# Load order, scratch of the cross products, and the last output rows of a gated long-convolution and MLP kernel

## The chip, the cores and the metric

The kernel runs on one core of one Trainium2 chip. The metric is device time in microseconds (us): the median of four runs, 191.75 us, with single runs from 191.6 to 191.89. Lower is better.

The core has a matrix engine (TensorE, PE in the profile; its weight loads are listed as PEld), VectorE (DVE), ScalarE (ACT), GpSimd (POOL), a queue engine that issues most transfers (SyncE, SP) and 16 DMA engines. Matrix products land in PSUM and are read from there by ScalarE or VectorE; everything else lies in SBUF.

## The reference

There are 2048 positions with 640 channels each. The output mixes two branches with a gate per position: `g * a + (1 - g) * b`.

```
g = sigmoid(sum(q * gate_w, channels))

# branch a: short filter, product, long convolution, product
k_shift = 4-tap causal filter of k over positions, own taps per channel
kv      = k_shift * v
y       = causal convolution of kv with ssm_k (2048 taps per channel) + kv * ssm_D
a       = q * y

# branch b: a two-layer MLP over the positions, per channel
h = layernorm(q over channels)
u = gelu(h^T @ w1 + b1)          # 2048 positions -> 1536
b = (u @ w2 + b2)^T              # 1536 -> 2048 positions
```

All inputs and the output are bf16. The reference does the long convolution by a Fourier transform of twice the length.

## The kernel before, in words

**Branch a.** The positions are split by residue: position 4r + p belongs to residue p, and the 2048 positions to four blocks `hk` of 512, two per half h. The long convolution is done in a transformed domain. TensorE multiplies the filter and the product kv by tables of sines and cosines (`FTB`, filled by ScalarE from integer angles that VectorE prepares in `pint`); ScalarE copies each result out of PSUM into a spectrum tile `C[0]` to `C[3]`, with `SS` as a further half tile. VectorE combines the residues (`mixing`), multiplies spectra, combines again (`invmix`), and TensorE multiplies by the transposed tables `GTB` (`inverse`). ScalarE scales the result by the gate into one of three `cgb` buffers; VectorE multiplies by q and adds the MLP branch, which is already in `O1`; a transfer stores the rows.

**The filter's way in.** `ssm_load(hk)` loads one 640 KB block of the filter, `x_load(hk)` one 640 KB block of q. `transp(h, p, kt)` transposes the filter on TensorE in 16 groups of five 128x128 products, and ScalarE evicts each to `wT`. The very first group also folds in the row `ssm_D`. `fwd` then makes the spectra from `wT`. The 4-tap filter's taps are transposed in a group named `cst`, evicted by ScalarE into `cw` in four pieces, and GpSimd makes `KF` from `cw`.

**Branch b.** Layer normalisation statistics and scaling of q are VectorE work (GpSimd supplies the reciprocal root). The first layer is 12 output tiles of 64 products (`m1`), each followed by a gelu on ScalarE; the second is 16 tiles of 24 products (`m2`), in the block order 2, 3, 0, 1. Each `m2` tile is evicted by ScalarE with scale `omg` (that is 1 - g) and bias `c2` (that is (1 - g) * b2) into `O1`. The very last tile (block 1, residue 3) goes through its first 320 channels before its last 320, so that the two halves can leave PSUM one after the other.

**The spectral products.** The product of half 1's output needs two terms: the cross product of half 1's data with half 0's filter and the other way round. `cross(g)` makes, for each of two spectra, a product into the scratch `T1` (the tile `tm[1]`), a temporary in `tm[0]`, two results in place, and a transfer on GpSimd's queue that adds the temporary into the first result while it moves. `y1(g)` calls `product`, which uses all of `tm[0]` (as `T0`) and `tm[1]` (as `T1`), and sends two more adding transfers. Half 0's two products follow with the same scratch. Before these, `mixing(C[3], C[2], 0)` works in place on `C[3]` and leaves the data in slots 2 and 3; slots 0 and 1 are later the scratch of half 1's `invmix` (`C3a`).

**What sets the order.** The program adds every operation to a planner (`_Sched`) in program order. The planner finds dependencies from the memory regions read and written. `run` then simulates the engines with fixed costs: an engine that is free takes the ready operation with the lowest `prio`, which is the operation's index unless one is given (0 means at once; `m1` and `m2` chunks of 8 products have very high numbers and fill gaps). Loads on one queue share one rate of 320 GB/s and are due 2 us after they have moved; the adding transfers on GpSimd's queue get 1.2 us to issue and 5 us after they have moved. Each PSUM tile is a `_VT`, which takes one of four PSUM slots from its first product to its last eviction; the convolution class may hold three, the MLP class two. An eviction that depends on something outside its tile hands that dependency to the tile's first product. The planned order is then written out, engine by engine, and a tracker adds the semaphore waits; on the chip the order of each engine is fixed, but the times are not the planner's. Loads marked `chain=True` keep program order.

Lines in the profile are mostly those of helpers: L293 is every matrix product, L666 every ScalarE operation, L622 every two-operand VectorE or GpSimd operation, L636 and L637 operations with a scalar, L870 and L872 the statistics, L267 plain transfers, L262 adding transfers, L260 transposing transfers. Tile names tell them apart (`pp` is PSUM).

Of the kernel before, what the change touches and what calls it, by code (L numbers as in the profile page):

```python
# [12 lines left out]
ACT = mybir.ActivationFunctionType  # L13
ALU = mybir.AluOpType
# [308 lines left out]
class _Sched:  # L323
# [171 lines left out]
    def emit(self):  # L495
        for op in self.order:
            op.emit(None if op.vt is None else self.slots[op.vt.slot])
# [12 lines left out]
def _build(nc, A_q, A_k, A_v, A_shift_k, A_ssm_k, A_ssm_D, B_x, B_w1, B_b1, B_w2, B_b2, gate_w, out):  # L510
# [10 lines left out]
    with ExitStack() as es:  # L521
# [8 lines left out]
        SC = _Sched(T, pp)  # L530
# [21 lines left out]
        def V(h, off, dims, p0=0, pn=128):  # L552
            row = T.mem[h.name][2]
            return bass.AP(tensor=h, offset=p0 * row + off, ap=[[row, pn]] + [list(d) for d in dims])
# [74 lines left out]
        def ts(eng, o, a, s1, s2, op0, op1=None, mode=1, prio=None, extra=0.0):  # L629
            n = n_of(o)  # L630
            d = dve_dur(n, mode) + extra if eng == "DVE" else n / 900.0 + 0.2
            rr = [a] + [x for x in (s1, s2) if isinstance(x, bass.AP)]

            def f(e):
                if s2 is None:
                    return e.tensor_scalar(o, a, s1, None, op0=op0)  # L636
                return e.tensor_scalar(o, a, s1, s2, op0=op0, op1=op1)  # L637
            o_ = SC.add(eng, d, lambda s: T.op(eng, f, rr, [o]), rr, [o], prio=prio, name="ts")
            o_.lock = eng == "POOL" or mode > 1
            return o_  # L640
# [8 lines left out]
        def act(o, i, func, bias=None, scale=None, acc=None, vt=None, prio=None, name="act"):  # L649
            kw = {}  # L650
            rr = []
            nap = 0
            for k_, v_ in (("bias", bias), ("scale", scale)):
                if v_ is not None:
                    kw[k_] = v_
                    if isinstance(v_, bass.AP):
                        rr.append(v_)
                        nap += 1
            ww = [o]
            if acc is not None:  # L660
                kw["accum_out"] = acc
                ww.append(acc)

            def emit(s):
                src = i(s) if vt is not None else i
                return T.op("ACT", lambda e: e.activation(o, src, func, **kw), rr + [src], ww)  # L666
            return SC.add("ACT", act_dur(n_of(o), nap), emit, rr if vt is not None else rr + [i], ww, prio=prio, vt=vt, name=name)

        def evac_dve(o, i, vt, prio=None):
# [2 lines left out]
                return T.op("DVE", lambda e: e.tensor_copy(o, src), [src], [o])  # L672
            return SC.add("DVE", dve_dur(n_of(o), 1), emit, [], [o], prio=prio, vt=vt, name="evd")

        def memset(eng, ap, val, prio=None):
            return SC.add(eng, 0.2, lambda s: T.op(eng, lambda e: e.memset(ap, val), [], [ap]), [], [ap], prio=prio)

# [29 lines left out]
        def dr(t, off, ap):  # L707
            return bass.AP(tensor=t.tensor, offset=t.offset + off, ap=ap)
# [7 lines left out]
        def chk(ci):  # L716
            return lambda s: s[:, ci * 512:ci * 512 + 320]

        def ssm_load(hk):
            dma(ssm[:, :, 512 * hk:512 * hk + 512], dr(A_ssm_k, 512 * hk, [[S, 128], [128 * S, ND], [1, 512]]), 128 * ND * 1024, chain=True)  # L720

        def x_load(hk):
            dma(X[:, hk, :, :], dr(A_q, 512 * hk * D, [[4 * D, 128], [1, 4 * D]]), 128 * 5120, chain=True)
# [23 lines left out]
        def small(o, i, nbytes, stream, **kw):  # L747
            dma(o, i, nbytes, stream=stream, **kw)
# [2 lines left out]
        small(rows[0:4, 1, :], dr(B_b2, 0, [[512, 4], [1, 512]]), 4096, "QA")  # L751
        small(rows[0:12, 2, 0:128], dr(B_b1, 0, [[128, 12], [1, 128]]), 3072, "QA")
        small(Drow[:, :], dr(A_ssm_D, 0, [[0, 1], [1, D]]), 1280, "QA")
        x_load(0)
        for hk in range(2):
            ssm_load(hk)
        for hk in range(1, 4):
            x_load(hk)
        ssm_load(2)
# [242 lines left out]
                        act(gb[:, b, :], gb[:, b, :], ACT.Copy, acc=gacc[:, t:t + 1], name="gsum")  # L1002

        tt("DVE", gth[:, :], sd[:, :], gacc[:, :], ALU.mult, mode=1, prio=0)
        ts("DVE", gpre[:, :], mv[:, :, 0], gws[:, 0:1], None, ALU.mult, mode=1, prio=0)
        tt("DVE", gpre[:, :], gpre[:, :], gth[:, :], ALU.add, mode=1, prio=0)
        act(gth[:, :], gpre[:, :], ACT.Tanh, scale=0.5, prio=0)
        ts("DVE", gg[:, :], gth[:, :], 0.5, 0.5, ALU.mult, ALU.add, mode=1, prio=0)
# [4 lines left out]
            dma(GTB[:, p, :, :, :, :].rearrange("q a b c d -> q (a b c) d"), FTB[:, p, :, :, :, :].rearrange("q a b c d -> q (a b c) d"), 128 * 2048, rate=200.0, transpose=True, prio=10 ** 5)  # L1013

        HORD = (2, 3, 0, 1)
        for kt in range(2):
            dma(q_hi[:, kt, :, :], dr(A_q, (1024 + 512 * kt) * D, [[4 * D, 128], [1, 4 * D]]), 128 * 5120)
        for n_, hk in enumerate(HORD):
            W2h = W2[n_ % 2]
            for a in range(2):  # L1020
                w2last = dma(W2h[:, 6 * a:6 * a + 6, :], dr(B_w2, a * 6 * 128 * S + 512 * hk, [[S, 128], [128 * S, 6], [1, 512]]), 128 * 6144)
            for p in range(4):
                vt = _VT("mlp")
                t = 4 * hk + p
                last_ = n_ == 3 and p == 3
                order = [(ft, ci) for ci in range(2) for ft in range(FT)] if last_ else [(ft, ci) for ft in range(FT) for ci in range(2)]
                na = 2 if last_ else 3
                for a in range(na):
                    items = []
                    for ft, ci in order[a * (24 // na):(a + 1) * (24 // na)]:  # L1030
                        items.append((chk(ci), V(W2h, ft * 512 + p, [[4, 128]]), GT[:, ft, 320 * ci:320 * ci + 320], ft == 0, ft == FT - 1))
                    mms(vt, items, prio=2 * 10 ** 6 + 4 * (4 * n_ + p) + a, name="m2")
                    if last_:
                        act(O1[:, hk, p, 320 * a:320 * a + 320], chk(a), ACT.Identity, bias=c2[:, t:t + 1], scale=omg[:, t:t + 1], vt=vt, name="o1")
                if not last_:
                    act(O1[:, hk, p, :].rearrange("p (a b) -> p a b", a=2), two, ACT.Identity, bias=c2[:, t:t + 1], scale=omg[:, t:t + 1], vt=vt, name="o1")

# [44 lines left out]
        def cross(g):  # L1082
            for i in range(2):
                n_ = ncr[0]
                ncr[0] += 1
                tmp = V(tm[0], 1280 * (n_ % 4), [[1, 1280]])
                tt("DVE", half(T1, n_ % 2), half(A0[g], i), half(V1[g], i, True), ALU.mult)
                tt("DVE", tmp, comp(A0[g], i, 1), comp(V1[g], i, 1), ALU.mult)
                tt("DVE", comp(V1[g], i, 0), comp(A0[g], i, 0), comp(V1[g], i, 0), ALU.mult)
                tt("DVE", comp(V1[g], i, 1), comp(T1, n_ % 2, 1), comp(T1, n_ % 2, 0), ALU.subtract)  # L1090
                dma(comp(V1[g], i, 0), tmp, 128 * 5120, stream="POOL", prio=0, accum=True)
# [24 lines left out]
        def inverse(h, Z):  # L1116
            for p in (0, 2, 1, 3):
                hz, sz = Z[p]
                cg = cgb[ncg[0] % len(cgb)]
                ncg[0] += 1  # L1120
                for kt in range(2):
                    t = 8 * h + 4 * kt + p
                    vt = _VT("cv")
                    items = []
                    for k2 in range(2):
                        for c in range(2):
                            for ci in range(2):
                                items.append((chk(ci), GTB[:, p, kt, c, k2, :], V(hz, sz * SL + (2 * c + k2) * D + 320 * ci, [[1, 320]]),
                                              k2 == 0 and c == 0, k2 == 1 and c == 1))
                    mms(vt, items, name="inv")  # L1130
                    act(cg[:, kt, :].rearrange("p (a b) -> p a b", a=2), two, ACT.Copy, scale=gg[:, t:t + 1], vt=vt, name="cg")
                ov = O1[:, 2 * h:2 * h + 2, p, :]
                tt("DVE", cg[:, :, :], cg[:, :, :], (q_lo if h == 0 else q_hi)[:, :, p, :], ALU.mult)
                if h == 0 and p == 3:
                    tt("DVE", O1[:, 0, p, :], cg[:, 0, :], O1[:, 0, p, :], ALU.add)
                    dma(dr(out, p * D, [[4 * D, 128], [1, D]]), O1[:, 0, p, :], 128 * 1280, sem="out")
                    for ci in range(2):
                        ov = O1[:, 1, p, 320 * ci:320 * ci + 320]
                        tt("DVE", ov, cg[:, 1, 320 * ci:320 * ci + 320], ov, ALU.add)
                    ov = O1[:, 1, p, :]  # L1140
                    dma(dr(out, (512 + p) * D, [[4 * D, 128], [1, D]]), ov, 128 * 1280, sem="out")
                else:
                    tt("DVE", ov, cg[:, :, :], ov, ALU.add)
                    dma(dr(out, (1024 * h + p) * D, [[4 * D, 128], [512 * D, 2], [1, D]]), ov, 256 * 1280, sem="out")
# [54 lines left out]
```

## Time and profile before

| | us |
|---|---|
| median of four runs | 191.75 |
| the profiled execution | 191.78 |
| its span, first to last instruction | 190.0 |
| TensorE busy | 176.2 |
| VectorE busy | 170.3 |
| ScalarE busy | 116.8 |
| GpSimd busy | 33.5 |

The profile shows one execution, so sums over it are made against 191.78 and 190.0. The granted TensorE clock was full throughout. "Busy" is an average over stages with different limits: an engine at 90% can still be off the path that sets the end, and what a change is worth has to be read from the stage in which it lies. An idle time in front of an instruction is put down to the semaphore that came last.

### The profile page before, as it was taken

The numbers are of one execution on the slowest core, as the hardware profiler recorded it, in microseconds if no ns is written. First come the engines' busy times: TensorE is split into PE (matmuls) and PEld (weight loads), VectorE is DVE, ScalarE is ACT, GpSimd is POOL, SyncE is SP. The second block draws the span as 40 slices with busy tenths as digits, with TensorE's granted clock in tenths as the row PEclk, the third lists the DMA queues.
The fourth block names the chain that finished last, engine by engine and source line by source line (L and its number), as shares of the span: only waits on it lengthen the run. The fifth ranks groups of instructions, "written<-read, shape, count | busy, mean of one in ns | idle before, by whom it ended". The sixth has DMA issues, their size and how long they took to land.

```text
span 190.0 us, 3364 instructions
## 1 busy us (share of the span) xinstructions
PE 176.2 (93%) x1403; PEld 131.5 (69%) x1403; DVE 170.3 (90%) x196; ACT 116.8 (61%) x187; POOL 33.5 (18%) x33
## 2 busy tenths in 40 slices
PE   0469998979999999999999999999999999999993
PEld 0356575648767877677777777888888886786782
DVE  7999968984999999999999979999999992999461
ACT  4898989899889997999422211131313138646552
POOL 2199031850004510001002201331000000000000
PEclk9999999999999999999999999999999999999999
DMA  5999999991799999998558835989956900412222
GB/s 185 358 397 348 392 247 213 339 419 77 120 166 335 258 205 245 306 278 208 104 127 254 167 59 164 285 167 181 246 175 202 385 25 0 141 69 71 72 104 104
DMA packets 37295, 38.93 MB, mean 205 GB/s; under 512 B 15643, under 2 KB 32672, under 8 KB 37280
## 3 DMA queue, kind: packets, MB, share of 16 engines
q1 hardware_dynamic: 34464, 32.15, 55.1%
q0 software_dynamic: 2752, 6.55, 19.3%
q8 instruction: 11, 0.18, 0.4%
q14 instruction: 4, 0.03, 0.0%
q10 hardware_dynamic: 64, 0.01, 0.0%
HBM read 25.87 MB, written 2.62 MB: 150 GB/s over the span
## 4 chain that ended last, share of the span: by engine, by line
PE 86%; ACT 8%; DMA 3%; issue 0%; SPq 0%; DVE 0%
PE pp L293 86%; ACT wT L666 3%; DMA ssm<-in_A_ssm_k_dram 3%; ACT C L666 3%; ACT FTB L666 1%; ACT L666 1%; ACT GT L666 0%; ACT O L666 0%; SPq L267 0%; DVE O L622 0%
## 5 line engine op out<-in xcount | busy, mean ns | idle before, releaser
L293 PE MATMUL pp<-X,ring 128*128 128x320 bf16 x384 | 54.1, 299 | 0.0
L293 PE MATMUL pp<-GT,W 128*128 128x320 bf16 x384 | 53.0, 299 | 0.0
L293 PEld LDWEIGHTS pp<-GT,W 128*128 128x128 bf16 x384 | 43.4, 114 | 9.0 <-issue 0.3
L622 DVE TENSOR_TENSOR C<-C 128x2560 bf16<-128x2560 bf16 (+1 forms) x28 | 49.1, 1774 | 0.0
L293 PEld LDWEIGHTS pp<-X,ring 128*128 128x128 bf16 x384 | 37.4, 98 | 14.4
L666 ACT ACTIVATE C<-pp 128x640 bf16<-128x640 f32 x64 | 39.5, 733 | 3.9 <-PE pp L293 3.9
L666 ACT ACTIVATE O<-pp,c,omg 128x640 bf16<-128x640 f32 (+1 forms) x17 | 14.5, 853 | 35.0 <-PE pp L293 35.0
L666 ACT ACTIVATE GT<-pp,cc 128x640 bf16<-128x640 f32 x12 | 9.6, 797 | 19.0 <-PE pp L293 19.0
L622 DVE TENSOR_TENSOR tm<-C,C 128x2560 bf16<-128x2560 bf16 (+2 forms) x12 | 20.1, 1713 | 1.1 <-DMA C<-tm 1.1
L293 PE MATMUL pp<-wT,FTB 128*128 128x320 bf16 x128 | 19.9, 310 | 1.3 <-ACT C L666 1.1
L293 PEld LDWEIGHTS pp<-wT,FTB 128*128 128x128 bf16 x128 | 11.6, 101 | 8.7 <-ACT C L666 3.3
L666 ACT ACTIVATE cgb<-pp,gg 128x640 bf16<-128x640 f32 x16 | 12.7, 792 | 5.6 <-PE pp L293 5.6
L622 DVE TENSOR_TENSOR C<-tm 128x2560 bf16<-128x2560 bf16 (+1 forms) x12 | 15.0, 1267 | 0.1
L262 POOL DMA_DIRECT2D C<-C x6 | 7.5, 1414 | 34.9 <-DVE C L622 34.9
L293 PE MATMUL pp<-C,GTB 128*128 128x320 bf16 x96 | 13.7, 299 | 0.0
L870 DVE BATCH_NORM_STATS2 stats<-X 128x6 f32<-128x320 bf16 x32 | 13.3, 452 | 0.0
L666 ACT ACTIVATE gq<-gq 128x640 bf16<-128x640 bf16 x16 | 12.0, 769 | 0.6 <-DVE gq L622 0.6
L293 PEld LDWEIGHTS pp<-C,GTB 128*128 128x128 bf16 x96 | 9.0, 98 | 4.2 <-ACT O L666 0.4
L622 DVE TENSOR_TENSOR tm<-C,SS 128x5120 bf16<-128x5120 bf16 x4 | 11.1, 2818 | 0.0
L666 ACT ACTIVATE wT<-pp 128x640 bf16<-128x640 f32 x16 | 10.1, 717 | 1.4 <-PE pp L293 1.4
L293 PE MATMUL pp<-ident,ssm 128*128 128x128 bf16 x80 | 8.2, 266 | 2.9 <-DMA ssm<-in_A_ssm_k_dram 1.9
L262 POOL DMA_DIRECT2D C<-tm x4 | 3.5, 866 | 37.8 <-DVE C L622 37.8
(64 smaller groups left out, 181.8 us busy)
## 6 DMA issues: line engine op xcount, KB each, us to landing
ring<-in_B_w_dram SPq DMA_DIRECT2D x12, 512.0 KB, 11.3
W<-in_B_w_dram SPq DMA_DIRECT2D x8, 768.0 KB, 6.6
C<-C POOLq DMA_DIRECT2D x6, 640.0 KB, 8.2
X<-in_A_q_dram SPq DMA_DIRECT2D x4, 640.0 KB, 8.8
ssm<-in_A_ssm_k_dram SPq DMA_DIRECT2D x4, 640.0 KB, 9.6
kn<-in_A_k_dram SPq DMA_DIRECT2D x4, 640.0 KB, 8.6
out_dram<-O SPq DMA_DIRECT2D x7, 320.0 KB, 2.3
vkv<-in_A_v_dram SPq DMA_DIRECT2D x2, 640.0 KB, 5.0
```

Source lines behind the costliest of these rows:

```text
L262: ins = engobj.dma_start(out_ap, in_ap, accum_op=ALU.add, max_dma_last_dim=2560)
L293: ins = self.nc.tensor.matmul(ps_ap, lhsT=lhsT, rhs=rhs, start=start, stop=stop, skip_group_check=True)
L622: o_ = SC.add(eng, d, lambda s: T.op(eng, lambda e: e.tensor_tensor(o, a, b, op), [a, b], [o]), [a, b], [o], prio=prio, name="tt")
L666: return T.op("ACT", lambda e: e.activation(o, src, func, **kw), rr + [src], ww)
L870: ops.append(SC.add("DVE", 0.38, (lambda o, i: lambda s: T.op("DVE", lambda e: e.bn_stats(o, i), [i], [o]))(o, i), [i], [o]))
```

## The change

1. Of the eight big loads at the front, the first filter block now comes first, then the first block of q, then the second filter block; the rest is as before.
2. The operation that makes `gpre` (mean of q times the sum of the gate weights) loses its priority 0 and takes its index.
3. In `cross`, the temporary lies in `C[3]`, slots 0 and 1, instead of `tm[0]`.
4. The last `m2` tile is no longer evicted by ScalarE. Instead VectorE adds `c2` to the gated convolution result of those rows, and two new operations (`last_stt`, one for each 320 channels) read PSUM, multiply by `omg` and add that sum, straight into `O1`. These are added to the planner at the end of `inverse(0)`, so the tile's first product also depends, in the plan, on the sum that they read.

```diff
+        def last_stt(o, i, sc, b, vt):
+            def emit(s):
+                src = i(s)
+                return T.op("DVE", lambda e: e.scalar_tensor_tensor(out=o, in0=src, scalar=sc, in1=b, op0=ALU.mult, op1=ALU.add), [src, sc, b], [o])
+            return SC.add("DVE", dve_dur(n_of(o), 1), emit, [sc, b], [o], vt=vt, name="fin")
...
+        ssm_load(0)
         x_load(0)
-        for hk in range(2):
-            ssm_load(hk)
+        ssm_load(1)
...
-        ts("DVE", gpre[:, :], mv[:, :, 0], gws[:, 0:1], None, ALU.mult, mode=1, prio=0)
+        ts("DVE", gpre[:, :], mv[:, :, 0], gws[:, 0:1], None, ALU.mult, mode=1)
...
+        lastvt = []
...
                     if last_:
-                        act(O1[:, hk, p, 320 * a:320 * a + 320], chk(a), ACT.Identity, bias=c2[:, t:t + 1], scale=omg[:, t:t + 1], vt=vt, name="o1")
+                        lastvt.append(vt)
...
-                tmp = V(tm[0], 1280 * (n_ % 4), [[1, 1280]])
+                tmp = V(C[3], 1280 * (n_ % 4), [[1, 1280]])
...
                     dma(dr(out, p * D, [[4 * D, 128], [1, D]]), O1[:, 0, p, :], 128 * 1280, sem="out")
+                    t = 4 + p
+                    ts("DVE", cg[:, 1, :], cg[:, 1, :], c2[:, t:t + 1], None, ALU.add, mode=2)
                     for ci in range(2):
-                        ov = O1[:, 1, p, 320 * ci:320 * ci + 320]
-                        tt("DVE", ov, cg[:, 1, 320 * ci:320 * ci + 320], ov, ALU.add)
+                        last_stt(O1[:, 1, p, 320 * ci:320 * ci + 320], chk(ci), omg[:, t:t + 1], cg[:, 1, 320 * ci:320 * ci + 320], lastvt[ci])
```

## The prediction

> **What bounds the kernel now.** I read the chain that ended last first, then a table by stage, then the waits, then the order of the single engines at the two ends. The chain gives TensorE 86% of the span. The stages, cut where the chain changes engine (stretch, length, then busy time and instructions of PE, PEld, DVE, ACT, POOL, then clock, DMA share and GB/s):
>
> ```profile
> 0.00:7.24 7.24, 0.27 (x4) 0.18 (x5) 6.23 (x15) 4.32 (x7) 1.21 (x10) 1.00 0.69 227
> 7.24:14.84 7.60, 5.68 (x48) 4.41 (x48) 7.60 (x27) 6.51 (x10) 6.01 (x3) 1.00 1.05 398
> 14.84:46.46 31.62, 29.84 (x248) 20.08 (x249) 25.88 (x53) 28.96 (x48) 12.88 (x9) 1.00 0.95 299
> 46.46:116.84 70.38, 70.38 (x592) 51.54 (x593) 69.21 (x58) 47.15 (x86) 8.56 (x8) 1.00 0.84 194
> 116.84:186.87 70.03, 70.01 (x514) 55.25 (x511) 61.01 (x46) 29.22 (x37) 4.87 (x4) 1.00 0.56 155
> 186.87:190.00 3.13, 0.00 (x0) 0.00 (x0) 0.33 (x1) 0.62 (x1) 0.00 (x0) 1.00 0.26 92
> ```
>
> From 46.46 to 186.87 us TensorE has no gap, so a saving on another engine there is worth nothing unless TensorE starts to wait. Time can be won before 46.46, where TensorE starts late, and after 186.87, where it has finished. The head, in the chain in order of time (start, length, what):
>
> ```profile
> 1.18 6.02 DMA ssm<-in_A_ssm_k_dram
> 7.24 0.74 PE pp L293 x5
> 8.00 1.30 ACT wT L666 x2
> 9.30 2.07 ACT FTB L666 x2
> 11.37 0.60 ACT wT L666
> 12.11 1.35 PE pp L293 x7
> ```
>
> The first filter block lands at 7.19; five transposes follow, and from 8.00 on ScalarE carries the chain. ScalarE's own order shows what it did before:
>
> ```profile
> 4.11 2.19 ACT L666 ACTIVATE FTB<-pint,cst 128x1024 bf16<-128x1024 int32 x2 [0.33 <-DVE pint L636]
> 6.21 1.01 ACT L666 ACTIVATE cw<-pp 32x80 bf16<-32x80 f32 x4
> 8.00 1.30 ACT L666 ACTIVATE wT<-pp 128x640 bf16<-128x640 f32 x2 [0.78 <-PE pp L293]
> 9.18 2.19 ACT L666 ACTIVATE FTB<-pint,cst 128x1024 bf16<-128x1024 int32 x2
> ```
>
> It is free at 7.22 and idles 0.78 us for the block. The two loads at the front of the queue (KB, us from issue to landing):
>
> ```profile
> X<-in_A_q_dram SPq DMA_DIRECT2D x1, 640.0 KB, 3.9
> ssm<-in_A_ssm_k_dram SPq DMA_DIRECT2D x1, 640.0 KB, 6.0
> ```
>
> The row block, issued at 0.72, lands at 4.6; the filter block, issued at 1.18, at 7.2. The tail, and VectorE's longest waits ahead of it:
>
> ```profile
> 186.89 0.62 ACT L666 ACTIVATE O<-pp,c,omg 128x320 bf16<-128x320 f32 x1 [1.01 <-PE pp L293]
> 187.54 0.33 DVE L622 TENSOR_TENSOR O<-cgb,O 128x320 bf16<-128x320 bf16 x1 [1.31 <-ACT O L666]
> ```
> ```profile
> DVE cgb L622 <- ACT cgb L666: 6.6, 4, 2.4
> DVE gpre L636 <- ACT gq L666: 3.3, 1, 3.3
> DVE tm L622 <- DMA C<-tm: 1.1, 1, 1.1
> ```
>
> [...]No VectorE instruction of this trace reads PSUM; [...]ScalarE evicts the first 320 columns at 185.26 while TensorE fills the other bank until 186.87. [...]7 forward products start in 15.0-16.0, 12 in 17.0-18.0.
>
> **The change, part by part.**
>
> *Loads.* The filter block goes from second to first; nothing is added and every later transfer keeps its place. It should land when the row block did, 4.6, or up to 1 us later, since its 1 KB rows moved more slowly (2.6 us between the two landings); I take 5.3. The row block then lands near 7.2, and its first reader, a VectorE statistic, starts at 8.09 behind table work: 0.9 us of cover. Without it every later VectorE step of the head, and the mask for POOL's filter product, moves by the lateness.
>
> The order on each engine is fixed by the kernel's planner; I worked its rule through by hand, for order alone. With the block due first, three transposes take all three convolution slots before the tap transposes can, so ScalarE gets: two FTB, two wT, four cw, two FTB, three wT. On the chip: first five transposes done at 5.3 + 0.74 = 6.1, ScalarE free at 6.21-6.3, two wT to 7.5 (1.3), four cw (1.0) to 8.5, two FTB (2.1) to 10.6; before, these two ended at 11.3. That is 0.7. The tap evictions end at 8.5 instead of 7.2; POOL's filter product, which needs them, started only at 8.83 behind the mask, so it is covered by 0.3. The transposes of the second block, landing at 9.1 as before, are done by 10.3. Next the folded group (1.35 us through TensorE) starts after two wT instead of one, but another group is evicted meanwhile, and the forward products, which waited for two evictions after it, wait for one: 0.7-0.8 survives. Then the cold array takes its share: before, it was slow from 14.84 to about 17.0. If that point is fixed in time, the 0.7 us of earlier start is spent at half rate, where a group takes about 1.07 instead of ScalarE's 0.60, and only 0.4 is left. I take 0.55, bounds 0 and 1.0. From 17 to 46 TensorE and ScalarE pass the chain between them; normalised rows (VectorE, done at 21.8 and 31.8) are wanted at 23.15 and 33.2, so VectorE, which doesn't move, stays covered by over 0.8.
>
> *gpre.* Losing priority 0, it drops behind VectorE work of lower index. The 3.3 us wait goes, but two multiplies and a copy later (about 44.7) the product with the shifted keys waits for their eviction, which ScalarE starts only at 45.29: all but 0.4-0.8 comes back. TensorE wants that product at 52.82, ready at 51.7. Worth 0; it costs nothing either, since its result is needed at 94.7.
>
> *Cross operands.* The temporaries move from the product's own scratch to C[3]. The 1.07 us wait before the product T0 goes. But C[3] is free only after its own mixing, so two temporaries and the subtraction of the first part move behind the mixing while one multiply comes forward: net two ops, 2 x 0.74 = 1.49 us, behind it; the mixing starts 0.6 us earlier (its last input is evicted at 86.21, it began at 86.93). VectorE at the first y1 combination: -0.6 + 1.49 - 1.07 = -0.2, and -0.75 with the head. The first tap-product transfer goes from 85 to about 97 on POOL's queue; nothing stands between there, and its reader starts at 118. All this is under TensorE's cover, if TensorE's order doesn't move. It does: the planner charged 5 us for that wait, so it will put the inverse block of half 1 earlier among the second-layer products. By hand: six chunks of 8 matmuls earlier (6 x 1.09 = 6.5), and VectorE's two later combines fall behind the first inverse operand. On the chip that operand was ready at 151.2 and TensorE took it at 155.96, 4.8 of slack. After: ready at 151.2 - 0.75 - 2 x 1.40 = 147.7; taken at 155.96 - 6.5 - 0.55 = 148.9. Slack 1.2. Half 0 by the same count keeps about 1. So 0, if my count holds within a chunk.
>
> *Last rows.* Removed: two ScalarE evictions (0.62) and two adds (0.33). Added: one add of the bias to 640 elements (0.44, as the 128x640 row normalisation takes), in VectorE's 0.91 us gap before 184.55, and two PSUM reads of 320 elements[...]. The first runs by 185.8, hidden under the second half's matmuls. After the last matmul: 0.65 + 0.33 = 0.98 becomes 0.49. Gain 0.49 (0.33 to 0.65). The outgoing transfer keeps its 2.1 us.
>
> *Sum.* Span 190.0 - 0.55 - 0.49 = 188.96. The profiled execution took 191.78, 1.78 around its span: 190.74. The median of the runs shown is 0.03 lower: **190.7**.
>
> **Rivals.**
> - *The head's gain does not arrive* (the block lands later than 6.3, or the cold phase and the slot order eat it): only the tail counts, 191.25. [...]against: 0.78 of plain idle on the chain.
> - *Slower: TensorE waits in the inverse blocks.* Place: before the first inverse product of each half. For it: the planner drops a 5 us delay of which the chip saw 1.07, and the slack falls from 4.8 to about 1.2. Eight chunks instead of six give 148.9 - 2.2 = 146.7, a wait of 1.0 there and as much at half 0: 190.7 + 2.0 = 192.7. It is slower than before once the waits pass 1.04 + 0.38 = 1.4 us in all. Against: the planner's work durations match the chip (1.41 against 1.40 per 2560-element op), and a chunk is only begun when its operand is due.
> - *Nothing moves*: both gains lost in a later wait; 191.75.
> - *More*: the block lands at 4.8 and the array warms early, 1.0 at the head and 0.6 at the tail: 190.1.
>
> **How the numbers follow.** Forecast 0.61 (190.2 to 191.2, from the bounds above); head lost 0.13; TensorE waits 0.16; nothing moves 0.03; more 0.07. The lower tail is cut at 190.0; the range goes up to 192.0, which takes in the lost head and half of the slower case. Within 0.2% (0.38 us) is about what a measurement of this kernel can't tell from no change. Faster: 0.61 + 0.07 + 0.10 of the lost head = 0.78. Same: 0.03 + 0.03 + 0.03 of small waits = 0.09. Slower: 0.13.
>
> **What would show it.** Right: the first filter block landing at 5-5.7, wT ahead of cw on ScalarE, no 0.78 idle, gapless TensorE from about 45.9; the VectorE wait on the tm transfer gone; inverse products of half 1 starting near 149 with no wait; one VectorE op of 0.45-0.5 after the last matmul. Wrong: TensorE idle before an inverse product, statistics waiting for the row block, the filter product on POOL starting after 9, or a slow array beyond 17.

## The result and the profile after

The changed kernel takes 191.62 us (median of 35 runs, 190.79 to 192.18); the kernel before, run beside it, takes 192.05 (median of 56, 191.31 to 192.94). The ratio is 0.9976, with an interval of 0.9965 to 0.9987. On the 191.75 of the prediction that is 191.29: faster by 0.46 us, where 1.05 was forecast. The sign is right and less than half of the size arrived.

The profiled execution took 191.49 with a span of 189.7 (191.78 and 190.0 before). Its table by stage, cut at the same times and with the same columns as before (second and third stage):

```profile
7.24:14.84 7.60, 4.77 (x40) 3.20 (x39) 7.60 (x27) 7.25 (x13) 6.00 (x3) 1.00 1.05 396
14.84:46.46 31.62, 29.88 (x248) 20.08 (x246) 27.05 (x54) 28.59 (x48) 12.84 (x9) 1.00 0.97 299
```

ScalarE does 0.74 us more in the second stage (7.25 for 6.51): the idle time before the first filter block is gone. But TensorE does no more than before in the third (29.88 for 29.84), and there the gain should have shown. The two loads at the front (KB, us to landing):

```profile
ssm<-in_A_ssm_k_dram SPq DMA_DIRECT2D x1, 640.0 KB, 4.9
X<-in_A_q_dram SPq DMA_DIRECT2D x1, 640.0 KB, 5.9
```

Issued at 0.72 and 1.24, they landed at 5.6 and 7.1; the forecast was 5.3 and 7.2. What TensorE and ScalarE then did, in order of time (start, length, operation, then the idle time before it and its releaser). TensorE:

```profile
5.62 1.79 PE L293 MATMUL pp<-ident,ssm 128*128 128x128 bf16 x15 [5.62 <-DVE pint L622]
7.34 0.28 PE L293 MATMUL pp<-ident,rows 20*128 20x20 bf16 x4
...
11.70 0.72 PE L293 MATMUL pp<-ident,ssm 128*128 128x128 bf16 x5 [1.40 <-ACT wT L666]
12.39 0.69 PE L293 MATMUL pp<-Drow,ident 1*128 1x512 bf16 x2
...
14.52 1.78 PE L293 MATMUL pp<-wT,FTB 128*128 128x320 bf16 x6
```

ScalarE:

```profile
6.38 1.30 ACT L666 ACTIVATE wT<-pp 128x640 bf16<-128x640 f32 x2
7.66 1.04 ACT L666 ACTIVATE cw<-pp 32x80 bf16<-32x80 f32 x4
8.72 2.19 ACT L666 ACTIVATE FTB<-pint,cst 128x1024 bf16<-128x1024 int32 x2
10.94 1.30 ACT L666 ACTIVATE wT<-pp 128x640 bf16<-128x640 f32 x2
12.46 2.60 ACT L666 ACTIVATE wT<-pp 128x640 bf16<-128x640 f32 x4 [0.22 <-PE pp L293]
```

The same place in the kernel before, TensorE:

```profile
12.11 0.69 PE L293 MATMUL pp<-Drow,ident 1*128 1x512 bf16 x2 [1.44 <-ACT wT L666]
```

Three readings. The second FTB pair starts at 8.72, against 9.18 before and 8.5 in the forecast. At 11.70 TensorE has waited 1.40 us for ScalarE (1.44 before), and the first group that it then does is an ordinary transpose of the second filter block; the folded group (`Drow`) comes only behind it, at 12.39, later than the 12.11 of before. And the first forward product (`wT,FTB`) starts at 14.52: 0.32 us earlier than before (14.84), not 0.7 to 0.8.

These 0.32 us are gone by the third eviction that follows. ScalarE's evictions of the first forward products, first in the kernel before, then in the changed one:

```profile
17.07 7.27 ACT L666 ACTIVATE C<-pp 128x640 bf16<-128x640 f32 x12 [0.24 <-PE pp L293]
```
```profile
16.87 0.70 ACT L666 ACTIVATE C<-pp 128x640 bf16<-128x640 f32 x1 [0.36 <-PE pp L293]
17.87 7.27 ACT L666 ACTIVATE C<-pp 128x640 bf16<-128x640 f32 x12 [0.29 <-PE pp L293]
```

The first eviction starts 0.31 us earlier than before (15.81 for 16.12), the second 0.20 earlier (16.87 for 17.07), the third 0.20 later (17.87 for 17.67, the second of the row of twelve above). In between, one more group of products ran at the slow pace: from 17.0 to 17.5 TensorE started two products in the changed kernel (0.27 us apart) and four in the kernel before (0.14 apart).

In the chain of work that ended last, the part of TensorE without a gap begins at 46.62, where before it began at 46.46. Nothing of the head is left. It ends at 187.02, and a single operation follows (start, length, what):

```profile
187.04 0.55 DVE O L678
```

The 1.00 us that followed the last product before are now 0.57 with the hand-over, 0.43 less. The bias add, 0.38 us at 182.26, lies in VectorE's idle time. VectorE's waits (us in all, times, the longest):

```profile
DVE cgb L622 <- ACT cgb L666: 5.9, 3, 3.4
...
DVE gq L622 <- ACT gq L666: 2.1, 1, 2.1
...
DVE vkv L622 <- ACT ksh L666: 1.0, 1, 1.0
```

The wait for the tm transfer is gone; that of `gpre` is gone too, with two others for ScalarE in its place. In TensorE's order, the inverse block of half 1 begins without a wait:

```profile
148.59 1.66 PE L293 MATMUL pp<-C,GTB 128*128 128x320 bf16 x11
```

### The profile page after: what moved, and what is told of

Its sections match the earlier page's. It is cut to its first block, busy times and chain, and to the rows that moved or that the text cites. A ratio compares the mean times of both kernels' runs of the same rounds, so it can differ in the third digit from the quotient of the medians.

```text
span 189.7 us, 3367 instructions
## 1 busy us (share of the span) xinstructions
PE 176.8 (93%) x1403; PEld 131.9 (70%) x1403; DVE 170.8 (90%) x197; ACT 116.1 (61%) x185; POOL 33.5 (18%) x33
## 4 chain that ended last, share of the span: by engine, by line
PE 88%; ACT 8%; DVE 3%; issue 0%; POOL 0%; POOLq 0%
PE pp L293 88%; ACT C L666 3%; ACT wT L666 2%; ACT FTB L666 1%; DVE pint L636 1%; DVE pint L622 1%; ACT L666 1%; ACT cw L666 0%; ACT GT L666 0%; DVE O L678 0%; DVE ident L636 0%; DVE rows L781 0%; POOL dif L773 0%; POOLq L773 0%; POOLq L1192 0%
## 5 line engine op out<-in xcount | busy, mean ns | idle before, releaser
L666 ACT ACTIVATE O<-pp,c,omg 128x640 bf16<-128x640 f32 x15 | 13.2, 883 | 27.7 <-PE pp L293 27.7
L262 POOL DMA_DIRECT2D C<-C x10 | 11.0, 1195 | 71.9 <-DVE C L622 40.5
L293 PE MATMUL pp<-wT,FTB 128*128 128x320 bf16 x128 | 20.5, 316 | 1.2 <-ACT C L666 1.1
L622 DVE TENSOR_TENSOR tm<-C,C 128x2560 bf16<-128x2560 bf16 (+1 forms) x8 | 17.0, 2155 | 0.0
L293 PEld LDWEIGHTS pp<-ident,ssm 128*128 128x128 bf16 x80 | 6.6, 128 | 10.6 <-DMA ssm<-in_A_ssm_k_dram 7.1
```

Source lines behind the costliest of these rows:

```text
L262: ins = engobj.dma_start(out_ap, in_ap, accum_op=ALU.add, max_dma_last_dim=2560)
L293: ins = self.nc.tensor.matmul(ps_ap, lhsT=lhsT, rhs=rhs, start=start, stop=stop, skip_group_check=True)
L622: o_ = SC.add(eng, d, lambda s: T.op(eng, lambda e: e.tensor_tensor(o, a, b, op), [a, b], [o]), [a, b], [o], prio=prio, name="tt")
```

## Experiments

The theory after the result: the tail pays its 0.43 to 0.49, the rest of the change pays nothing, and the head's gain is lost partly to the order in which the planner now puts TensorE's and ScalarE's work there, partly to the slow array (the prediction's cold array: the phase in which TensorE starts a product of 320 columns every 0.27 us, as from 15.08 to 16.68 in the trace of the kernel before, and not every 0.14, as there from 16.87 on). The rivals: the head does pay, and something else takes it back (the cross products, or a wait in an inverse block); or the slow array alone eats it. Ratios are to the kernel before on the same chip, where its median was 191.87 to 191.92.

**The last rows alone.** Kernel before with part 4 of the change.

```diff
-                        act(O1[:, hk, p, 320 * a:320 * a + 320], chk(a), ACT.Identity, bias=c2[:, t:t + 1], scale=omg[:, t:t + 1], vt=vt, name="o1")
+                        lastvt.append(vt)
...
+                        last_stt(O1[:, 1, p, 320 * ci:320 * ci + 320], chk(ci), omg[:, t:t + 1], cg[:, 1, 320 * ci:320 * ci + 320], lastvt[ci])
```

> Only the last output rows are formed from PSUM; load order, scratch and priority as before. Theory A (the tail is all of the gain, the head's earlier start is spent while the array runs at half rate): 0.43 us faster, ratio 0.9978, as the whole change. Theory B (the head's gain is real and another part gives it back): also 0.43 faster here, but then the load order alone must be 0.4 or more faster too. Profile: one VectorE operation of about 0.55 us after the last product, TensorE ends where it did.

Measured 191.69 (22 runs), ratio 0.9985 [0.9969, 1.0000], a gain of 0.29 us with an interval down to nothing. In its profile TensorE ends at 186.78 and one operation of 0.55 follows, as in the whole change. That agrees with the tail's price, but these runs spread over 1.5 us and don't fix it; a pair below does.

**The load order alone.** Kernel before with part 1.

```diff
+        ssm_load(0)
         x_load(0)
-        for hk in range(2):
-            ssm_load(hk)
+        ssm_load(1)
```

> Only the load order is changed. Theory A: the first spectrum eviction is about 0.3 us earlier than before, the array is slow until the same time, and the gain in the end is 0 to 0.2 us (ratio 0.999 to 1.000). Theory B: 0.4 us or more faster (ratio 0.998 or less). Theory C (the planner's new order on ScalarE, with wT waiting for its slot, eats the gain already): the first spectrum eviction is not earlier than in the kernel before.

Measured 192.19 (22 runs), ratio 1.0011 [0.9997, 1.0024]: not faster. Its chain shows a wait that neither whole kernel has:

```profile
168.63 0.80 ACT cgb L666
...
172.33 2.89 DVE SS L622 x2
...
175.48 0.80 ACT cgb L666
176.33 11.10 PE pp L293 x80
```

In half 0's inverse block the chain leaves TensorE: from 46.65 to 187.44 it took 140.79, where the kernels without this wait take 140.39 to 140.41. So TensorE waited about 0.4 us there, brought about by the loads alone. That is akin to my slower rival but not at its place: what waited at 176.33 is a group of the second layer, for ScalarE's `cgb`, and not the first inverse product for its operand. The whole change does not have this wait, so it explains this kernel and not the result. One profile shows it.

**Cross products and `gpre` alone.** Kernel before with parts 2 and 3.

```diff
-        ts("DVE", gpre[:, :], mv[:, :, 0], gws[:, 0:1], None, ALU.mult, mode=1, prio=0)
+        ts("DVE", gpre[:, :], mv[:, :, 0], gws[:, 0:1], None, ALU.mult, mode=1)
...
-                tmp = V(tm[0], 1280 * (n_ % 4), [[1, 1280]])
+                tmp = V(C[3], 1280 * (n_ % 4), [[1, 1280]])
```

> Only the temporaries of the cross products move to C[3] and gpre loses its priority; load order and tail as before. If these two are worth nothing, as predicted, because TensorE has no gap there: ratio 1.000 (0.999 to 1.001), no wait of VectorE on the tm transfer, inverse products earlier and no TensorE wait before them. If the new order makes TensorE wait: 0.3 to 1 us slower.

Measured 191.86 (14 runs), ratio 1.0002 [0.9985, 1.0019]; TensorE runs without a gap from 46.55 for 140.40. They neither pay nor cost.

**The change without its load order.** The changed kernel with the loads of before.

```diff
-        ssm_load(0)
         x_load(0)
-        ssm_load(1)
+        for hk in range(2):
+            ssm_load(hk)
```

> The changed kernel with the load order of before. If the load order brings nothing while the array is slow at the start: as fast as the changed kernel, 0.43 us faster than before (ratio 0.9977). If the load order brings 0.2 to 0.3: 0.2 slower than the changed kernel, ratio 0.999. If the load order costs time: faster than the changed kernel.

Measured 191.41 (14 runs), ratio 0.9965 [0.9949, 0.9981]. The change as it stands has 0.9976 [0.9965, 0.9987]. Without part 1 it is no slower: as made, the new load order brings nothing that these runs show.

**A busy array, first try.** Does the slow array eat the head's gain? In the kernel before and in the changed one, 59 products of the identity with itself go where TensorE waits anyway before 14 us. They are of no use to the result and land in a PSUM tile that nothing reads yet.

```diff
+                for _ in range(FILL.pop(0) if FILL else 0):
+                    T.mm(pp[3][:, 0:128], ident[:, :], ident[:, :], True, True, fv, False)
                 for k_, (o, l, r, st, sp) in enumerate(items):
```

> The kernel before, with 59 products of the identity with itself put into TensorE's early waits (30, 14, 3 and 12 of them, into the PSUM slot that nothing uses before 22 us), so that the array is busy from about 1.6 us on. Theory A: forward products run at full rate from the first, about 0.27 us less per group of four for the groups that were slow; 0.6 to 1.2 us faster than before (ratio about 0.995), and the times of single runs lie within 0.5 us instead of 1.6. If the slow phase is not what decides: no change, or slower by the products that don't fit into the waits.

> The changed kernel with 59 such products in its own early waits (36, 11 and 12). Theory A: with the array at full rate the earlier start comes through, so it is 0.3 (start) + 0.43 (tail) = 0.7 to 0.9 us faster than the kernel before with its waits filled. Theory C or B: only 0.43 faster than that kernel, the tail alone.

Measured: before with filling 190.21 (15 runs), ratio 0.9935 [0.9910, 0.9961]; the change with filling 190.82 (13 runs), 0.9918 [0.9887, 0.9948]. The medians mislead, since the runs of both lie in two groups: 190.09 to 190.27 (nine) and 191.04 to 192.37 (six) for the first, 189.43 to 189.68 (six) and 190.82 to 191.66 (seven) for the second. The recorded clock parts them in the same way: every run of the two upper groups lists a mean granted clock of 0.991 or 0.982, every run of the lower groups at least 0.997. So the filling sometimes did what it was for, and then paid over 1.5 us. The lower groups differ by about 0.69 us, which is not explained by the tail alone.

**A busy array, second try.** Products of 512 columns each, in the same kind of places: 29 in the kernel before, 28 in the changed one.

```diff
+                    T.mm(pp[3][:, 0:512], ident[:, :], V(ident, 0, [[0, 4], [1, 128]]), True, True, fv, False)
```

> The kernel before with 28 products of 512 columns of no use (the identity with itself, four times over) in TensorE's early waits and one in front of each group up to the first forward products, denser than the 59 short ones. Theory (the slow phase sets the spread and the level): every run falls into the fast group of the kernel with 59 short ones, 190.1 to 190.3, 1.7 us faster than before (ratio 0.991), spread under 0.4 us.[...]

> The changed kernel with 28 such products. If the earlier start comes through with the array at full rate: 189.4 to 189.6 in every run, 0.7 us faster than the kernel before filled in the same way (0.43 for the tail and 0.26 for the start), ratio to the kernel before 0.9875. If only the tail counts: 189.75.

Measured: before with them 190.42 (6 runs, 190.30 to 190.63), ratio 0.9908 [0.9888, 0.9929]; the change with them 189.92 (6 runs, 189.61 to 190.28), 0.9880 [0.9856, 0.9904], slower than was expected of the tail alone (189.75). Here the runs of each lie within 0.7 us. TensorE in half a microsecond (stretch, length, busy with the instructions that run in it or reach into it, granted clock, DMA share, GB/s), first in the changed kernel, then in the kernel before with dense filling:

```profile
16.50:17.00 0.50, 0.50 (x4) 1.00 1.11 352
```
```profile
16.50:17.00 0.50, 0.50 (x6) 1.00 1.10 348
```

Six products instead of four fall in the same time, under the same recorded clock; with dense filling the first 52 forward products of the kernel before take 7.59 us, 0.15 each. With the fast array the kernel before reaches its gapless part at 44.98 instead of 46.46: the slow phase costs 1.5 us. The change with it reaches that part at 45.13, no earlier. But its first forward product has no head start there: it starts at 14.44, that of the kernel before at 14.24. So on a fast array the new order takes the whole gain before the forward products, and this pair does not tell what took the 0.32 us that were left on the slow one.

**The change without its load order, dense.** To split the 0.50 between those two.

> The changed kernel without its load order, with those products. If the load order as it was made brings nothing with a fast array either: as fast as or up to 0.2 us faster than the changed kernel filled in the same way, 0.43 under the kernel before filled in the same way: 189.8 to 190.0. If the load order is worth 0.26 there: 190.15 to 190.2.

Measured 189.94 (6 runs, 189.88 to 190.08), ratio 0.9889 [0.9866, 0.9913], equal to the 189.92 with the load order. So on a fast array, too, the load order as made shows no gain; the runs with it lie over 0.67 us, so that a few tenths either way are not excluded. The rest of the change is worth 190.42 - 189.94 = 0.48. Since parts 2 and 3 are worth nothing, that is the tail.

**The change with the head's order given back.** The transposes of the first filter block are made to follow the tap group, and two groups of the second block and the constants to follow the folded group. The loads stay as the change has them.

```diff
-        mms(vt, items, prio=0, name="cst")
+        cst_op = mms(vt, items, prio=0, name="cst")
+        first = []
...
-            mms(vt, items, name="cst")
+            mms(vt, items, name="cst").after.add(first[0])
...
-            mms(vt, items, name="wtr")
+            m = mms(vt, items, name="wtr")
+            if hk == 0:
+                m.after.add(cst_op)
+            if dfold:
+                first.append(m)
+            if hk == 1 and p in (1, 3):
+                m.after.add(first[0])
```

> The changed kernel with the head's order of before given back: the filter's first transposes stay behind the tap group, and the folded group stays ahead of the two transposes that the new due times let past it. The loads keep their new order. If the new order was what cost the start (cw after wT, a slot wait of 0.2, the folded group last): the second pair of FTB starts at 8.5 instead of 8.7, the first forward product at about 14.1 instead of 14.5, before it was 14.8. The time: at most 0.2 us under the changed kernel, because the slow array takes the rest (ratio to before 0.9965 to 0.9976).

Measured 190.75 (8 runs, 190.25 to 191.62), ratio 0.9931 [0.9906, 0.9957]: faster than the change as made (0.9976), the intervals apart, and by more than the 0.2 us expected at most. Against the change without its load order (0.9965 [0.9949, 0.9981]) the intervals overlap, so what the load order is then worth on the slow array is not fixed. TensorE's order in this kernel:

```profile
11.37 0.69 PE L293 MATMUL pp<-Drow,ident 1*128 1x512 bf16 x2 [0.86 <-ACT wT L666]
...
14.10 2.32 PE L293 MATMUL pp<-wT,FTB 128*128 128x320 bf16 x8
```

The folded group starts 1.02 us earlier than in the change as made, the first forward product 0.42 earlier. Against the kernel before that product is 0.74 earlier, as the prediction had it. But the gapless part starts at 46.27, only 0.19 earlier: in this profile 0.55 went while the array was slow.

**The same on a fast array.** Dense products added to it (26).

> The same with the 512-column products in TensorE's early waits. If order and slow array together took the earlier start: first forward product at about 13.6 instead of 14.44 in the changed kernel filled in the same way, and 0.5 to 0.8 us under it: 189.2 to 189.4. If the load order can't bring anything even so: 189.9 as that kernel.

Measured 189.41 (5 runs, 189.39 to 189.41), ratio 0.9861 [0.9837, 0.9884]; the fastest version made, and faster than both kernels. Its first forward product starts at 13.84 and its gapless part at 44.53. With the old load order on a fast array these were 14.35 and 45.08. Here the 0.51 us that the first forward product gains are all there at the gapless part (0.55) and in the time: 189.94 - 189.41 = 0.53.

## Why the prediction was right and wrong

**Loads: the step that failed.** It went wrong at "0.7-0.8 survives" and so at "I take 0.55". At the first forward product 0.32 us had survived, at the gapless part nothing, and the times show nothing (0.46 us in all, 0.25 to 0.67 by the interval, of which the tail is 0.43 to 0.48). Two things took it:

- *The order in the head.* I had worked out rightly that two wT would go ahead of the four cw, and that the folded group would come after two wT. But I had put the FTB pair 0.7 us earlier, and it came 0.46 earlier. The block landed at 5.6 where I had 5.3 (its slower 1 KB rows show in the trace of the kernel before: packets of 1 KB moved at 275 to 285 GB/s from 3.9 to 5.6 us, those of 5 KB at 384 to 391 from 2.7 to 3.9), so the first wT began at 6.38 and not at 6.21; wT, cw and FTB then ran one behind the other without idle time. From the pair's end to the first forward product I had counted on no loss; it took 3.61 us (10.91 to 14.52), in the kernel before 3.47 (11.37 to 14.84). With the old order given back and the loads left new, the pair starts at 8.44, these 3.47 us return, and the first forward product comes at 14.10, which is my 0.74. On a fast array this order makes the same loads worth 0.53 us where they were worth nothing.
- *The slow array.* I had named it, with 0.4 left "if that point is fixed in time". It was not fixed: in the profile of the change the pace rises 0.75 us later than before (the last step of 0.27 us ends at 17.43, before at 16.68), and the 0.32 us are gone by the third eviction. In that of the change with the order given back, 0.19 of 0.74 was left, and four products still fall in 17.0 to 17.5, where the kernel before has six; with dense products all of the gain came through. These are single profiles. (The prediction's 7 and 12 products are sums over half microseconds, in which one that reaches over a border counts twice; 4 start in 15.0 to 16.0 and 8 in 17.0 to 18.0.) The prediction's half rate is measured as 0.27 against 0.14 us from start to start, and dense products took the slow phase away from the forward products (five or six fall in every half microsecond from 14.5 to 18.5). The two profiles with sparse filling record a clock of 0.50 for 3.4 us each, and a mean clock of 0.991 over 190 us is the same loss, 1.7 us, or 3.4 at 0.50. What sets the moment at which the pace rises was not shown.

The change as made lost to both on the slow array; on a fast one the order alone took everything (14.44, against 14.24 and 14.35 with the old loads). My rival "the head's gain does not arrive" named both the slot order and the cold phase, and gave 191.25 against the measured 191.29. It had a chance of 0.13. I had set 0.78 us of idle time against it, and that idle time did go. The waits that remain in front of the folded group and the later wT (1.40 and 0.22 us) are no longer than those of before (1.44 and 0.33), so it was not a new wait that ate the gain. Removed idle time is a gain only if what follows keeps its order and its pace.

**Last rows: right.** Forecast 0.49; 0.43 in the profile, 0.48 on the fast array, 0.29 with an interval down to nothing on the slow one. The PSUM read took 0.55 us where I took 0.49. That figure was assumed: no trace of before has such a read, only the add of 320 elements in SBUF (0.33) and ScalarE's eviction of 320 (0.62, 0.65 with the hand-over). The measured 0.55 lies between these. The bias add cost nothing on the path.

***gpre*: right.** Worth 0; the wait of 3.3 us went and came back as 2.1 and 1.0.

**Cross operands: right, in part by luck.** Worth 0 (1.0002 [0.9985, 1.0019]), and no TensorE wait before an inverse product in the whole change. The count of chunks was exact for this part: with the old loads (cross products and `gpre` alone) 240 second-layer products stand before half 1's first inverse product instead of 288, six chunks of 8. There the first y1 combination ran 0.16 us earlier than before, in a profile whose gapless part began 0.09 later: near the forecast 0.2. In the whole change it ran 0.76 earlier, at 114.01, where 0.75 was forecast; but 0.55 of that was to be the head's gain, which did not come. Most of it came with the new loads all the same (114.66 in the change without them): with them the last products with kv stand two chunks of first-layer products earlier in TensorE's order (the last starts at 83.26, before at 85.19). And half 1's inverse block, forecast at 148.9, starts at 148.59, because with the new loads it was moved by seven chunks (232) and not by six. Its operand is ready at about 147.5 (two operations of 1.40 from 144.70), forecast 147.7. The slack is 1.1 where I had 1.2, so the slower rival did not occur in the whole change. The wait of 0.4 us with the load order alone shows that such waits can arise from a changed order; it is not in the changed kernel and decided nothing there. (What the prediction calls the first tap-product transfer is the adding transfer of the first cross product; it went at 98.52, forecast about 97.)

**What stays open.** The 0.69 between the lower groups of the sparse filling, against 0.50 between the dense kernels, rests on few runs. So does what the load order as made is worth on a fast array: its two lowest runs there (189.61, 189.65) lie 0.3 below those without it. With the order given back the times gained more over the change as made (0.0045 of 191.75, 0.86 us) than its profile (0.35); the intervals, taken at their ends, allow 0.15 to 1.55, and the profiled run, 191.15, is the second slowest of its eight (median 190.75). Why the change of pace moved to 17.5 in the profiles with the new load order was not tried.

## To carry to other kernels

When a planner fixes the order, a load that is made due earlier changes which work takes the scarce slots first: follow by name each group up to the one that the path waits for, and if it has slipped, pin the order with an explicit dependency. In this kernel, whose TensorE starts in short bursts, dense products without use in its early waits were worth more than the tuning around them (1.5 us against 0.46), and they made small differences measurable (runs over 0.02 to 0.7 us instead of 1.6). The last tile left PSUM through the engine that would have followed anyway, everything else summed before, and that was worth 0.43 us.

## What the runs showed of the hardware

The slow phase often does not show in the granted clock: most profiles record 1.00 while products of 320 columns start 0.27 us apart instead of 0.14 (in the kernel before from 15.08 to 16.68 and from 16.87 on), and so the "full throughout" of the kernel before says nothing of its pace there. It can be seen in the pace of equal operations instead: five transposes take 0.74 us in it (the kernel before, at 7.24) and 0.44 outside (the same with dense products, at 7.21). Of the profiles kept, the two with sparse filling recorded it, 0.50 from about 14.1 to 17.5 us in the one and 13.8 to 17.2 in the other (worked out from the means of half microseconds at the ends: 0.56 and 0.52, 0.79 and 0.80). With sparse filling the mean clock of a run tells its group: at least 0.997 in the fast ones, 0.991 in most of the slow ones, and 0.982, twice the loss, in the slowest of each kernel (192.37; 191.50 and 191.66). Without filling it tells little: 0.991 stands in 8 of the 59 runs of the kernel before that were made beside the first experiments, at 191.68 to 191.88, near their median.

The filling changed the spread as well as the time. The runs of the kernel before lie over 1.6 us; with dense products over 0.3, in the changed kernel with them over 0.7, without its load order over 0.2, and in the version with the order given back over 0.02. The 59 short products, which amount to about half the columns, gave two groups of runs instead.
